# Low-rank attention followed by a maxout feed-forward on one Trainium2 core: the first batch's v in four loads, sums and copies in another order, the last product in narrower pieces

## The chip, the cores and the metric

The kernel runs on one core of one Trainium2 chip. A core has five engines with instruction queues of their own: TensorE (PE, with its weight loads shown apart as PEld), VectorE (DVE), ScalarE (ACT), GpSimd (POOL) and SyncE (SP). They meet through semaphores. DMA transfers are issued here by POOL (all loads of inputs) and by SP (E and F, the transposing transfers, and all stores). The metric is the device time of one execution in microseconds (us), given as the median of several runs.

## What is computed

For each of 8 batches and 8 heads, k and v (1024 rows of 64) are first projected to 64 rows with E and F; then comes ordinary softmax attention of q over those 64 rows. The result, as x with 8192 rows of 512, goes through a feed-forward layer with a two-way maximum:

```python
k_proj = np.einsum('ks,bhsd->bhkd', E, k)
v_proj = np.einsum('ks,bhsd->bhkd', F, v)
scores = scale * np.matmul(q, k_proj.transpose(0, 1, 3, 2))
attn = softmax(scores)
x = np.matmul(attn, v_proj)          # then heads side by side: 8192 x 512
g = np.maximum(x @ w1, x @ w2)       # 8192 x 1024
out = g @ w_out                      # 8192 x 512
```

## The kernel before

The maximum is taken as `max(x w1, x w2) = relu(x (w1 - w2)) + x w2`, so that `out = relu(x Wd) w_out + x (w2 w_out)`. `Wd = w1 - w2` (the tile `wd_sb`) and `M = w2 w_out` (the tile `m_sb`) are made once, while batch 0 is worked on; `M` is built by `m_steps`, seven products p1, p2, p6, p5, p7, p3, p4 with the additions of a Strassen-Winograd scheme. The same scheme with seven products is used for the two large products of every unit. A unit is half of a batch (512 rows), so there are 16 of them, numbered 0 to 15. `up_steps` makes `relu(x Wd)` of a unit in the tile `gt`; `down_steps` makes the unit's output. The scheme needs sums of blocks of its left operand: `sums_x` (of x) and `sums_g` (of gt), both at L590 and on DVE, and differences of blocks of its right operand (`T_sb`, L481, DVE, and `step_tw`).

Nothing is scheduled automatically. The order of the work on each engine is the order in which the program calls the steps: first the opening (batch 0's attention, written out line by line at the end), then a list `slots`, in which the up pieces of one unit alternate with the down pieces of the unit before. `at_slot(key, step, ...)` hangs further steps behind a slot. Slots (0, 10) to (0, 15) are the last up pieces of batch 0, slots (0, 16) to (0, 22) the seven steps of `m_steps`. Every engine works its own queue in order.

Loads of batch 0 are issued by POOL in this order: k, q, k, q of the first four heads and then of the last four, two heads at a time (L101); v, four heads at a time; then w2 and w1 in pieces (L124 and L133), `w_out` (L137), and batch 1's k, v, q and batch 2's k.

`step_kv` projects k or v with `eft`, the transposed E and F. For v of batch 0 it is called once for heads 0 to 3 and once for heads 4 to 7; each projection is written twice, to the lower and the upper 64 partitions of one PSUM bank. For batches 3 to 7 it is called for k and v of all heads together, and returns `finish_v`, which runs after the next slot: DVE copies v (L203), doubles the projected k (L205), SP then issues a transposing DMA that makes `kpt` (L230), and DVE copies v to the other half (L207). POOL waits on the doubled k (`step_gate`, L236) before it issues the loads of the next batch.

In the last unit (number 15) nothing runs beside the down products. There p4 is made in two halves of 128 output rows, each with an addition at L779 and a store of its own at L726.

Of the kernel before, what the change touches and what calls it, by code (L numbers as in the profile page):

```python
# [12 lines left out]
ALU = mybir.AluOpType  # L13
# [3 lines left out]
def kernel(  # L17
# [12 lines left out]
    nc = tc.nc  # L30

    B, H, S, D = q.shape
    KP = E.shape[0]
# [25 lines left out]
    def mm_bank(dtype=FP32, n=None):  # L59
        if n is None:  # L60
            n = turn.pop(0)
            turn.append(n)
        return ps.tile([128, 512 if dtype == FP32 else 1024], dtype, tag=f"mm{n}", name="mm_ps")
# [36 lines left out]
    def load(t, n, src, b, h0, h1):  # L100
        nc.gpsimd.dma_start(  # L101
            out=t[n][:, h0:h1],
            in_=src[b, h0:h1].rearrange("h (p c) d -> p h c d", c=NC),
        )
# [4 lines left out]
    for h0 in (0, H // 2):  # L109
# [3 lines left out]
        if h0 == 0:  # L113
            ident = const.tile([128, 128], FP32)
            make_identity(nc, ident)
    load(tiles[0], "v", v, 0, 0, H // 2)
    load(tiles[0], "v", v, 0, H // 2, H)

    w1_sb = big(1).rearrange("p (r f) -> p r f", r=NDC)
    w2_sb = big(2).rearrange("p (r f) -> p r f", r=NDC)  # L120
# [58 lines left out]
    def step_kv(t, h0=0, h1=H, which="kv", att=False, dma=False, copy=nc.vector.tensor_copy):  # L179
        kv_ps = att_banks()[:, 0, :] if att else mm_bank()  # L180
        n = (h1 - h0) * D
        both = which == "v"
        for c in range(NC):
            for w in which:
                i = "kv".index(w)
                for r in range(2) if both else (i,):
                    nc.tensor.matmul(  # L187
                        out=kv_ps[r * KP : (r + 1) * KP, 0:n],
                        lhsT=eft[:, i, c, :],
                        rhs=t[w][:, h0:h1, c, :],  # L190
                        start=(c == 0), stop=(c == NC - 1),
                    )
        fl = lambda ap: ap[:, h0:h1].rearrange("p h z d -> p (h z d)")
        zd = lambda ap: ap.rearrange("p (h d z) -> p h z d", d=D // 2, z=2)
        if "k" in which:
            eng = nc.vector.tensor_copy if which == "k" else nc.scalar.copy
            kp = t["kp"][:, h0:h1]
            eng(out=kp[:, :, 0, :], in_=kv_ps[0:KP, 0:n].rearrange("p (h d) -> p h d", d=D))
        if both:
            copy(out=t["vp"][:, h0:h1], in_=zd(kv_ps[:, 0:n]))  # L200
        elif "v" in which:
            def finish_v():
                nc.vector.tensor_copy(out=t["vp"][KP:128, h0:h1], in_=zd(kv_ps[KP:128, 0:n]))  # L203
                if dma:
                    nc.vector.tensor_copy(out=kp[:, :, 1, :], in_=kp[:, :, 0, :])  # L205
                    step_kpt_dma(t)
                nc.vector.tensor_copy(out=fl(t["vp"][0:KP]), in_=fl(t["vp"][KP:128]))  # L207

            if att:
                return finish_v  # L210
            finish_v()
# [17 lines left out]
    def step_kpt_dma(t):  # L229
        nc.sync.dma_start_transpose(  # L230
            out=t["kpt"], in_=t["kp"].rearrange("p h r d -> p (h r d)")
        )
# [226 lines left out]
    NX = NDC // 2  # L459
    CH = DM // 2  # L460
    units = [(b, o) for b in range(B) for o in range(2)]
    U = {(b, o): {"n": n, "b": b, "o": o, "t": tiles[b]} for n, (b, o) in enumerate(units)}

    T_sb = const.tile([128, 4, NG + NX, CH], FP16)
# [109 lines left out]
    def x_blk(u, j, h):  # L574
        return u["t"]["xt"][:, h * NX : (h + 1) * NX, j, u["o"] * W : (u["o"] + 1) * W]

    def g_blk(u, j, h):
        if u["b"] == 0:
            return u["t"]["gt", u["o"]][:, h * NG : (h + 1) * NG, j * W : (j + 1) * W]
        return u["gt"][:, h * NG : (h + 1) * NG, j * W : (j + 1) * W]  # L580
# [30 lines left out]
    def up_steps(u):  # L611
        for d in range(2):
            st = {}
            xbank, ybank = (2, 3) if d == 0 else (3, 2)

            def product(k, name, n, st=st, d=d):
                if n is not None:
                    st[name] = mm_bank(n=n)
                bank = st[name]
                X = lambda j, h: x_blk(u, j, h)  # L620
                Wb = lambda h, c: wd_sb[:, h * NX : (h + 1) * NX, c * HALF : (c + 1) * HALF]
                S = lambda i: s_x(i, u)
                a, w_ = {
                    1: lambda: (X(0, 0), Wb(0, 0)), 2: lambda: (X(0, 1), Wb(1, 0)),
                    3: lambda: (S(3), Wb(1, 1)), 4: lambda: (X(1, 1), t_w(3)),
                    5: lambda: (S(0), t_w(0)), 6: lambda: (S(1), t_w(1)), 7: lambda: (S(2), t_w(2)),
                }[k]()
                for m in range(2):
                    for n_ in range(NX):
                        nc.tensor.matmul(  # L630
                            out=bank[:, m * W : (m + 1) * W],
                            lhsT=w_[:, n_, (2 * d + m) * 128 : (2 * d + m + 1) * 128],
                            rhs=a[:, n_, :],
                            start=(n is not None and m == 0 and n_ == 0),
                            stop=(n_ == NX - 1), skip_group_check=True,
                        )
                return bank

            two = lambda ap: ap.rearrange("q (m n) -> q m n", m=2)

            def c_blk(j, c, d=d):
                return u["gt"][:, c * NG + 2 * d : c * NG + 2 * d + 2, j * W : (j + 1) * W]

            def add(j, c, x, y, c_blk=c_blk):
                nc.vector.tensor_tensor(out=c_blk(j, c), in0=two(x), in1=two(y), op=ALU.add)  # L645

            def relu(ap):
                nc.vector.tensor_scalar_max(ap, ap, 0.0)  # L648

            def p1(st=st, product=product, xbank=xbank, d=d):  # L650
                if d == 0:
                    new_gt(u)
                st["s1"] = keep("pu", product(1, "X", xbank))

            def p2(st=st, product=product, ybank=ybank, add=add, c_blk=c_blk):
                add(0, 0, product(2, "Y", ybank), st["s1"])
                relu(c_blk(0, 0))

            def p6(st=st, product=product):
                st["u1"] = keep("pu", product(6, "X", None))  # L660

            def p5(st=st, product=product, ybank=ybank):
                st["s5"] = keep("pu", product(5, "Z", ybank))

            def p7(st=st, product=product):
                st["u2"] = keep("pu", product(7, "X", None))

            def p3(st=st, product=product, add=add, d=d):
                add(0, 1, product(3, "Z", None), st["u1"])
                add(1, 1, st["u2"], st["s5"])  # L670
                relu(u["gt"][:, NG + 2 * d : NG + 2 * d + 2, :])

            def p4(product=product, c_blk=c_blk):
                bank = product(4, "X", None)
                UP_C21(out=c_blk(1, 0), in_=two(bank))

            yield from (p1, p2, p6, p5, p7, p3, p4)
# [6 lines left out]
    def down_steps(u, alone):  # L684
# [36 lines left out]
        def o_tile():  # L721
            return opool.tile([128, 2, CH], FP32, tag="o", name="o_sb")

        def store(j, c, o_sb, i0=0, i1=2):
            def issue():
                nc.sync.dma_start(  # L726
                    out=out.rearrange("(n p i o) m -> n o p i m", p=128, i=NI, o=2)[
                        b, j, :, 2 * o + i0 : 2 * o + i1, c * CH : (c + 1) * CH
                    ],
                    in_=o_sb[:, i0:i1],  # L730
                )

            if u["n"] < 2:
                held.append(issue)
            else:
                issue()
# [36 lines left out]
        def p4():  # L773
            o_sb = o_tile()
            if alone:
                for i in range(2):
                    bank = product(4, ("C", i), 2 + i, 6 * i, 6 * i + 6)
                    part = slice(i * CH, (i + 1) * CH)
                    nc.vector.tensor_tensor(  # L779
                        out=o_sb[:, i], in0=bank[:, part], in1=st["u2"][:, part], op=ALU.add,  # L780
                    )
                    store(1, 0, o_sb, i, i + 1)
                return
            nc.scalar.copy(out=o_sb, in_=two(whole(4, "X", None)))
            store(1, 0, o_sb)
# [87 lines left out]

    last = len(units) - 1
    for n, key in enumerate(units):
        downs = down_steps(U[key], n == last)
        if n in (0, last):
# [21 lines left out]

    for key, s_, *a in (
        *((10 + i // 2, sums_m, i) for i in range(4)), *((12 + i, step_t, 0, (i,)) for i in range(4)),
        (15, open_box, 0, 1, 2), (16, sums_x, U[0, 0], range(4)),
        (18, sums_g, U[0, 0], (0, 1)), (19, sums_g, U[0, 0], (2, 3)), (22, open_box, 3),
    ):
        at_slot((0, key), s_, *a)
# [123 lines left out]
```

## Time and profile before

| | |
|---|---|
| median of 5 runs | 324.71 us (324.42 to 326.69) |
| the profiled execution's own time | 324.86 us |
| its span, from the first to the last instruction | 323.1 us |
| TensorE clock granted | 1.0 throughout |
| PE busy | 314.8 us, 97% of the span |
| DVE busy | 236.7 us, 73% |
| ACT busy | 208.2 us, 64% |
| POOL busy | 42.1 us, 13% |

The span is 1.8 us shorter than the execution's own time; the rest lies around it. In a list of instructions in order of time, each line gives the start in us, the duration in us, the engine, the line of the kernel, the operation and its tiles; in brackets stands how long the engine was idle before and what ended the wait. The waits are given as the total in us, the number of times, and the longest. A busy share is an average: a share of 97% says nothing of where the rest was lost.

### The profile page before, as it was taken

What the parts mean: (1) busy time and instruction counts of PE and PEld (TensorE: products, weight loads), DVE (VectorE), ACT (ScalarE), POOL (GpSimd) and SP (SyncE); (2) the same over time, 40 slices, a digit from 0 to 9 for tenths busy, and PEclk for the clock granted to TensorE, in tenths of its full rate; (3) what the DMA queues carried; (4) which work ended last, traced back from release to release, by engine and by line L of the source; (5) the groups of instructions that cost most, each with busy time, mean ns of one, the idle gap of its engine ahead of it and who ended that gap; (6) DMA issues with size and microseconds to landing.
All of it is one profiled execution on the core that took longest, in us unless ns stands there. A gap on an engine that the chain in (4) does not pass through costs nothing.

```text
span 323.1 us, 9062 instructions
## 1 busy us (share of the span) xinstructions
PE 314.8 (97%) x3872; PEld 250.4 (77%) x3872; DVE 236.7 (73%) x419; ACT 208.2 (64%) x373; POOL 42.1 (13%) x65
## 2 busy tenths in 40 slices
PE   8979999999999999999999999999999999999995
PEld 3545587777887888878887888878887888888884
DVE  1356798886967796877967796977967796969572
ACT  1476842767776777667776777657776777765541
POOL 8649002003000400021000400030000000000000
PEclk9999999999999999999999999999999999999999
DMA  8999999998959999899989899889969131213033
GB/s 151 203 200 184 202 205 204 207 191 132 207 110 163 170 202 245 200 202 165 231 192 208 165 204 245 204 166 188 225 131 213 36 100 34 97 34 100 32 122 108
DMA packets 76280, 53.14 MB, mean 164 GB/s; under 512 B 29520, under 2 KB 76112, under 8 KB 76240
## 3 DMA queue, kind: packets, MB, share of 16 engines
q0 software_dynamic: 30976, 28.31, 55.9%
q1 hardware_dynamic: 45264, 24.25, 31.1%
q8 instruction: 30, 0.49, 0.6%
q14 instruction: 10, 0.08, 0.1%
HBM read 57.15 MB, written 16.78 MB: 229 GB/s over the span
## 4 chain that ended last, share of the span: by engine, by line
PE 84%; DMA 8%; POOL 4%; DVE 3%; issue 1%; ACT 0%; DVEq 0%; POOLq 0%
PE mm_ps L710 45%; PE mm_ps L630 26%; DMA v_sb<-in_v_dram 4%; PE att_ps L187 4%; DMA wo_sb<-in_moe_w_out_dram 3%; PE att_ps L285 3%; PE mm_ps L273 3%; POOL big L133 2%; PE mm_ps L518 1%; POOL q_sb L101 1%; POOL k_sb L101 1%; DVE T_sb L481 1%; DVE gt_sb L645 1%; PE mm_ps L244 1%; DVE big L590 1%
## 5 line engine op out<-in xcount | busy, mean ns | idle before, releaser
L604 ACT COPY p_sb<-mm_ps 128x512 f32<-128x512 f32 x180 | 102.0, 593 | 47.1 <-PE mm_ps L630 30.0
L710 PEld LDWEIGHTS <-big 128*128 128x128 f16 x768 | 73.4, 98 | 12.4 <-issue 3.9
L710 PE MATMUL mm_ps<-T_sb,big 128*128 128x256 f16 x576 | 78.0, 273 | 0.0
L645 DVE TENSOR_TENSOR gt_sb<-mm_ps,p_sb 128x512 f16<-128x512 f32 x56 | 38.5, 688 | 45.4 <-PE mm_ps L630 41.6
L630 PE MATMUL mm_ps<-big,big 128*128 128x256 f16 x336 | 50.4, 273 | 0.0
L630 PEld LDWEIGHTS <-big 128*128 128x128 f16 x448 | 43.8, 98 | 5.4 <-issue 0.2
L710 PEld LDWEIGHTS <-gt_sb 128*128 128x128 f16 x384 | 35.9, 98 | 9.4 <-issue 5.0
L710 PE MATMUL mm_ps<-wo_sb,gt_sb 128*128 128x256 f16 x256 | 43.0, 273 | 0.1
L630 PEld LDWEIGHTS <-wd_sb 128*128 128x128 f16 x336 | 32.9, 98 | 4.2 <-issue 0.4
L630 PE MATMUL mm_ps<-xt_sb,wd_sb 128*128 128x256 f16 x224 | 33.6, 273 | 0.2 <-ACT ex_sb L366 0.2
L366 ACT ACTIVATE ex_sb<-mm_ps 128x512 f16<-128x512 f32 x50 | 27.2, 596 | 9.7 <-PE att_ps L285 7.6
L392 DVE TENSOR_TENSOR xt_sb<-att_ps,ld_sb 128x1024 f16<-128x1024 f32 x26 | 31.7, 1218 | 0.1
L740 DVE TENSOR_TENSOR o_sb<-mm_ps,p_sb 128x512 f32<-128x512 f32 x32 | 21.9, 684 | 7.0 <-PE mm_ps L710 6.9
L236 POOL COPY junk<-qt_sb 1x1 f16<-1x1 f16 x6 | 1.5, 257 | 176.8 <-DMA qt_sb<-q_sb 176.8
L710 PE MATMUL mm_ps<-m_sb,xt_sb 128*128 128x256 f16 x128 | 24.4, 273 | 0.0
L680 ACT ACTIVATE gt_sb<-mm_ps 128x512 f16<-128x512 f32 x28 | 16.8, 600 | 9.5 <-PE mm_ps L630 9.5
L590 DVE TENSOR_TENSOR big<-gt_sb 128x1024 f16<-128x1024 f16 x32 | 21.9, 685 | 0.2
L648 DVE TENSOR_SCALAR gt_sb<-gt_sb 128x512 f16<-128x512 f16 (+1 forms) x56 | 20.5, 365 | 1.9
L710 PE MATMUL mm_ps<-T_sb,gt_sb 128*128 128x256 f16 x128 | 21.5, 273 | 0.0
L710 PE MATMUL mm_ps<-wo_sb,big 128*128 128x256 f16 x128 | 21.5, 273 | 0.0
L710 PEld LDWEIGHTS <-xt_sb 128*128 128x128 f16 x192 | 18.8, 98 | 2.2
L645 DVE TENSOR_TENSOR gt_sb<-p_sb 128x512 f16<-128x512 f32 x28 | 19.1, 681 | 0.0
(98 smaller groups left out, 430.2 us busy)
## 6 DMA issues: line engine op xcount, KB each, us to landing
out_dram<-o_sb SPq DMA_DIRECT2D x63, 256.0 KB, 2.8
k_sb<-in_k_dram POOLq DMA_DIRECT2D x7, 1024.0 KB, 9.7
v_sb<-in_v_dram POOLq DMA_DIRECT2D x7, 1024.0 KB, 15.9
q_sb<-in_q_dram POOLq DMA_DIRECT2D x5, 1024.0 KB, 22.8
q_sb<-in_q_dram POOLq DMA_DIRECT2D x4, 512.0 KB, 18.8
big<-in_moe_w_dram POOLq DMA_DIRECT2D x12, 128.0 KB, 8.4
k_sb<-in_k_dram POOLq DMA_DIRECT2D x4, 256.0 KB, 6.3
q_sb<-in_q_dram POOLq DMA_DIRECT2D x4, 256.0 KB, 7.4
```

The source lines that it names most:

```text
L187: nc.tensor.matmul(out=kv_ps[r * KP : (r + 1) * KP, 0:n], lhsT=eft[:, i, c, :], rhs=t[w][:, h0:h1, c, :], start=(c == 0), stop=(c == NC - 1),)
L273: nc.tensor.matmul(out=banks[e][pos : pos + Z, h * W : (h + 1) * W], lhsT=t["kpt"][o * D : (o + 1) * D, head, s * Z : (s + 1) * Z], rhs=t[ ...
L366: nc.scalar.activation(out=t["ex", g, j][:, e, :], in_=banks[e], func=ACTF.Exp, scale=scale)
L392: nc.vector.tensor_tensor(out=x_out(t, g, j).rearrange("q z o n -> q o z n"), in0=at_ps.rearrange("q o (z n) -> q o z n", z=2), in1=ld[:, ...
L590: nc.vector.tensor_tensor(out=S(i), in0=S(0) if x is None else x, in1=y(), op=op)
L604: copy(out=x, in_=bank)
L630: nc.tensor.matmul(out=bank[:, m * W : (m + 1) * W], lhsT=w_[:, n_, (2 * d + m) * 128 : (2 * d + m + 1) * 128], rhs=a[:, n_, :], start=(n ...
L645: nc.vector.tensor_tensor(out=c_blk(j, c), in0=two(x), in1=two(y), op=ALU.add)
L648: nc.vector.tensor_scalar_max(ap, ap, 0.0)
L680: nc.scalar.activation(out=out, in_=in_, func=ACTF.Relu)
L710: nc.tensor.matmul(out=bank[:, i * CH : (i + 1) * CH], lhsT=a(c)[:, i * 128 : (i + 1) * 128], rhs=w_(c), start=(n is not None and m == (lo ...
L740: nc.vector.tensor_tensor(out=o_sb, in0=two(x), in1=two(y), op=ALU.add)
```

## The change

Six edits. v of batch 0 is loaded two heads at a time, and `step_kv` projects v of batch 0 two heads at a time. In `finish_v` the doubling of k and the transposing DMA come ahead of the first copy of v. In the last unit the relu over the two lower blocks is made in two parts, one after each addition. The last unit's p4 makes its second half in two pieces of 128 columns, so that it has three additions and three stores. Two of the four sums of x of unit 0 are called at slot (0, 11), where they stood at slot (0, 16), and the other two at slot (0, 17).

```diff
-    load(tiles[0], "v", v, 0, 0, H // 2)
-    load(tiles[0], "v", v, 0, H // 2, H)
+    for h in range(0, H, 2):
+        load(tiles[0], "v", v, 0, h, h + 2)
...
-        for c in range(NC):
-            for w in which:
-                i = "kv".index(w)
-                for r in range(2) if both else (i,):
-                    nc.tensor.matmul(
-                        out=kv_ps[r * KP : (r + 1) * KP, 0:n],
-                        lhsT=eft[:, i, c, :],
-                        rhs=t[w][:, h0:h1, c, :],
-                        start=(c == 0), stop=(c == NC - 1),
-                    )
+        nh = 2 if both else h1 - h0
+        for h in range(0, h1 - h0, nh):
+            for c in range(NC):
+                for w in which:
+                    i = "kv".index(w)
+                    for r in range(2) if both else (i,):
+                        nc.tensor.matmul(
+                            out=kv_ps[r * KP : (r + 1) * KP, h * D : (h + nh) * D],
+                            lhsT=eft[:, i, c, :],
+                            rhs=t[w][:, h0 + h : h0 + h + nh, c, :],
+                            start=(c == 0), stop=(c == NC - 1),
+                        )
...
             def finish_v():
-                nc.vector.tensor_copy(out=t["vp"][KP:128, h0:h1], in_=zd(kv_ps[KP:128, 0:n]))
                 if dma:
                     nc.vector.tensor_copy(out=kp[:, :, 1, :], in_=kp[:, :, 0, :])
                     step_kpt_dma(t)
+                nc.vector.tensor_copy(out=t["vp"][KP:128, h0:h1], in_=zd(kv_ps[KP:128, 0:n]))
                 nc.vector.tensor_copy(out=fl(t["vp"][0:KP]), in_=fl(t["vp"][KP:128]))
...
                 add(0, 1, product(3, "Z", None), st["u1"])
+                if u["n"] == last:
+                    relu(c_blk(0, 1))
+                    add(1, 1, st["u2"], st["s5"])
+                    relu(c_blk(1, 1))
+                    return
                 add(1, 1, st["u2"], st["s5"])
                 relu(u["gt"][:, NG + 2 * d : NG + 2 * d + 2, :])
...
-                for i in range(2):
-                    bank = product(4, ("C", i), 2 + i, 6 * i, 6 * i + 6)
-                    part = slice(i * CH, (i + 1) * CH)
+                a = cat(g_blk(u, 1, 1), x_blk(u, 1, 1))
+                for i, m0, m1, n in (0, 0, CH, 2), (1, 0, CH // 2, 3), (1, CH // 2, CH, xbank):
+                    bank = mm_bank(n=n)
+                    for c in range(NG + NX):
+                        nc.tensor.matmul(
+                            out=bank[:, 0 : m1 - m0],
+                            lhsT=a(c)[:, i * 128 : (i + 1) * 128],
+                            rhs=T_sb[:, 3, c, m0:m1],
+                            start=(c == 0), stop=(c == NG + NX - 1),
+                        )
                     nc.vector.tensor_tensor(
-                        out=o_sb[:, i], in0=bank[:, part], in1=st["u2"][:, part], op=ALU.add,
+                        out=o_sb[:, i, m0:m1], in0=bank[:, 0 : m1 - m0],
+                        in1=st["u2"][:, i * CH + m0 : i * CH + m1], op=ALU.add,
                     )
-                    store(1, 0, o_sb, i, i + 1)
+                    store(1, 0, o_sb, i, i + 1, m0, m1)
...
-        (15, open_box, 0, 1, 2), (16, sums_x, U[0, 0], range(4)),
+        (11, open_box, 1), (11, sums_x, U[0, 0], (0, 1)),
+        (15, open_box, 0, 2), (17, sums_x, U[0, 0], (2, 3)),
```

`open_box(1)` takes over the memory of `w1` for the sums of x; `open_box(0, 2)` that of E and F and of `w2`.

More of the change, by code (lines that the diff above doesn't have):

```diff
@@ L461 @@
     units = [(b, o) for b in range(B) for o in range(2)]
+    last = len(units) - 1
     U = {(b, o): {"n": n, "b": b, "o": o, "t": tiles[b]} for n, (b, o) in enumerate(units)}
@@ L666, in p7, with p3 @@
                 st["u2"] = keep("pu", product(7, "X", None))
-            def p3(st=st, product=product, add=add, d=d):
+            def p3(st=st, product=product, add=add, c_blk=c_blk, d=d):
                 add(0, 1, product(3, "Z", None), st["u1"])
+                if u["n"] == last:
[3 more added lines that the diff above has]
+                    return
                 add(1, 1, st["u2"], st["s5"])
@@ L722, in o_tile, with store @@
             return opool.tile([128, 2, CH], FP32, tag="o", name="o_sb")
-        def store(j, c, o_sb, i0=0, i1=2):
+        def store(j, c, o_sb, i0=0, i1=2, m0=0, m1=CH):
             def issue():
@@ L727, in issue @@
                     out=out.rearrange("(n p i o) m -> n o p i m", p=128, i=NI, o=2)[
-                        b, j, :, 2 * o + i0 : 2 * o + i1, c * CH : (c + 1) * CH
+                        b, j, :, 2 * o + i0 : 2 * o + i1, c * CH + m0 : c * CH + m1
                     ],
-                    in_=o_sb[:, i0:i1],
+                    in_=o_sb[:, i0:i1, m0:m1],
                 )
@@ L872 @@
     slots = [((0, n), x) for n, x in slots]
-    last = len(units) - 1
     for n, key in enumerate(units):
```

## The prediction, made before the changed kernel was run

> **What bounds the kernel now.** I read the page's totals first, then busy time by stretches, then the waits, then the order of time where PE has gaps.
>
> ```profile
> PE 314.8 (97%) x3872; PEld 250.4 (77%) x3872; DVE 236.7 (73%) x419; ACT 208.2 (64%) x373; POOL 42.1 (13%) x65
> ```
>
> ```profile
> core 0: us, PE busy (x) PEld busy (x) DVE busy (x) ACT busy (x) POOL busy (x), PEclk, DMA share, GB/s
> ...
> 20.00:28.00 8.00, 6.93 (x123) 3.91 (x120) 6.66 (x12) 3.96 (x7) 6.14 (x10) 1.00 1.38 196
> 42.00:50.00 8.00, 7.41 (x69) 5.98 (x69) 7.49 (x14) 2.93 (x5) 0.00 (x0) 1.00 1.32 203
> 150.00:310.00 160.00, 159.90 (x1967) 134.22 (x1965) 124.15 (x221) 110.62 (x204) 6.85 (x12) 1.00 0.72 149
> ```
>
> PE is busy 159.90 us of the 160 us from 150 on: there nothing can be won without removing matmuls, and the change removes none. Only the opening, one hole at 42 us and the tail are left. The hole, as PE and DVE see it in order of time:
>
> ```profile
> 41.27 1.04 PE L518 MATMUL mm_ps<-T_sb,p_sb 128*128 128x256 f16 x8
> 42.90 1.91 PE L518 MATMUL mm_ps<-T_sb,p_sb 128*128 128x256 f16 x16 [0.59 <-DVE m_sb L531]
> ```
>
> ```profile
> 38.16 0.69 DVE L481 TENSOR_TENSOR T_sb<-wo_sb 128x1024 f16<-128x1024 f16 x1 [1.20 <-DMA wo_sb<-in_moe_w_out_dram]
> ...
> 40.09 0.68 DVE L481 TENSOR_TENSOR T_sb<-wo_sb,T_sb 128x1024 f16<-128x1024 f16 x1
> 40.70 0.42 DVE L590 TENSOR_TENSOR big<-xt_sb 128x512 f16<-128x512 f16 x1
> ...
> 41.83 0.42 DVE L590 TENSOR_TENSOR big<-xt_sb,big 128x512 f16<-128x512 f16 x1
> 42.16 0.69 DVE L531 TENSOR_TENSOR m_sb<-mm_ps,p_sb 128x512 f16<-128x512 f32 x1
> ```
>
> DVE idles 1.20 us for `w_out`, makes four differences, then four sums of x, and only then p2's addition, which frees the bank that p5 needs. PE waits for it. The opening, from POOL's list and the DMA issues:
>
> ```profile
> 19.39 0.72 POOL L133 DMA_DIRECT2D big<-in_moe_w_dram x1 [2.93 <-DMA v_sb<-in_v_dram]
> 21.92 2.15 POOL L133 DMA_DIRECT2D big<-in_moe_w_dram x3 [1.82 <-DMA v_sb<-in_v_dram]
> ```
>
> ```profile
> v_sb<-in_v_dram POOLq DMA_DIRECT2D x2, 512.0 KB, 12.4
> ```
>
> Each of POOL's loads, from the ninth on, waits for the landing of the load eight before it (the eleventh on q's first, the seventeenth on v's first). And the tail:
>
> ```profile
> 310.71 0.43 DVE L648 TENSOR_SCALAR gt_sb<-gt_sb 128x1024 f16<-128x1024 f16 x1
> 311.24 0.69 DVE L590 TENSOR_TENSOR big<-gt_sb 128x1024 f16<-128x1024 f16 x1
> ...
> 311.96 0.69 DVE L590 TENSOR_TENSOR big<-big,gt_sb 128x1024 f16<-128x1024 f16 x1
> ...
> 312.71 5.13 PEld L710 LDWEIGHTS <-big 128*128 128x128 f16 x48 [0.22 <-DVE big L590]
> ```
>
> In the last unit relu, sum and sum follow one another on DVE, and PE's p6 waits for the end of them.
>
> **The change part by part.**
>
> *Two sums of x sooner.* At slot 11 they fall into DVE's 1.20 us of idling before 38.16: two at 0.42 us, overlapping by 0.07, are 0.78 us. Cover: the wait for `w_out`; without it they would cost 0.78 us on DVE. The other two go behind p2's addition. DVE is then free at 40.77. The addition also needs ACT's copy of p1 (done 41.19) and p2, whose last matmul ends at 41.44 (40.40 plus eight at 0.109, plus 0.17 of pipeline). It starts at 41.47 and ends at 42.16; p5 starts at 42.20 in place of 42.90. **-0.70 us.** What is late next? DVE: sums_x 2 and 3 run to 42.95, the four sums of gt (0.61 apart) to 45.5, so p3's addition comes at 45.5 in place of 45.79 while PE gained 0.70. p2's addition of unit 0 (50.32) comes 0.2 sooner, and PE's p5 needs it only after p6 (50.95 plus 1.31, less 0.70): covered by 0.8. Then the landing of batch 1's v: issued 28.84, 19.4 us under way, it lands at 48.24; its projection starts at 49.10 and can come at most 0.84 sooner.
>
> *v in four loads, projected by twos.* POOL issues two more, at 0.72 us each, ahead of all weights: the first weight load goes from 9.34 to 11.89, the next three each take the place two later. Their landings (9.34 plus 12.9, 10.61 plus 12.3, 11.89 plus 11.7, 13.23 plus 11.1) stand 0.65 us apart where the issues stand 1.3 apart: the transfers queue, so the landing does not move with the issue. From the fourth L133 load on, which waits for the last piece of v at 21.63, POOL's times stay, and with them `w_out` at 26.96. Cover: that queue. Projection: the first pair of heads (landing about 1.3 us before the whole half) is done while the second is under way, so each projection ends half of its 0.87 us sooner, -0.43 us. DVE is busy without a gap from 21.28 to 26.82, but fourth in it stands wd's difference at 23.08, which needs w1's first load, landed 22.91. So the three products before it start 0.43 sooner, and the rest only 0.14: **-0.14 us** at 27.41, where PE's unbroken run begins.
>
> Here a rule speaks against the change. The nearest rows: 16 transposes of 128 columns (L244) take 1.06 us, about 56 ns each, and 16 of 64 columns into two column groups (L218) 0.44 us, 27 ns each. The Trainium skill (TensorE: Matmul & The Clock Gate, Back-to-back issue gap) gives about 81 ns per matmul of 128 columns in a real stream of weight loads and matmuls. By the rows the 32 matmuls of a half take 0.9 us, as 16 do now. By the page 2.6 us: from 18.87 they end at 21.5 in place of 20.2, and 1.2 us is lost in the opening, of which the hole at 42 gives back 0.76; the last product loses 12 x 25 = 0.3. The whole sum is -0.65 by the rows, +0.95 by the page. I take the rows.
>
> *k doubled ahead of v.* Per batch, five times: the doubling (0.29) and the transposing DMA start 0.69 sooner on DVE and SP, the copy of v 0.29 later; the sum is the same. PE waited for `kpt` once, and that cost 0.03 us (the run before it ends at 217.79, the scores start at 217.81). vp is read 3 us later, the bank is wanted at 109.66 and free at 106.7. On SP only stores stand behind it. POOL's gate opens up to 0.69 sooner, and the next loads with it, but the transposing DMA has moved by the same. 0, between -0.05 and +0.3 (a kpt late once per batch by the 0.7 us that its landing varies, less slack 0.4).
>
> *Relu in two.* Addition 309.38, relu of 512 (0.29) at 310.10, addition 310.32, relu 311.04, sum at 311.43 in place of 311.24: **+0.19 us** before p6, which has no slack. What it buys, gt's first block ready sooner for p2 at 311.19, was in time anyway. In the first half of that unit (302.85) DVE idles afterwards: 0.
>
> *Last product.* Twelve matmuls at 56 ns for six at 109: 0. The last addition shrinks from 0.42 to about 0.29 (the relu and copies of half size: 0.29), but DVE and SP (0.36 to 0.44 per issue, now five in a row) bring the last issue to 320.0, against 319.93. It decides nothing: the stores run at about 340 GB/s without a gap from 319.05 to 321.5, the last 768 KB queueing behind one another. No row has stores in pieces of 512 bytes; bounds are -0.13 (all of the shorter addition) and +0.39 (128 KB at half of that rate). Loads that write 512-byte pieces (L124, 0.65 us per 128 KB) keep the rate of 1-KB ones (1.28 per 256 KB): 0.
>
> Sum: -0.70 - 0.14 + 0.19 = **-0.65 us**, on the profiled execution's 324.86: 324.21. That execution lies 0.15 above the median of 324.71, so the median should become **324.1**.
>
> **The rivals.**
>
> *A, the gain is stopped.* If batch 1's v lands 0.8 us later than here, the projection at 49.10 stays where it is and only the relu's +0.19 is left: 324.9. For: one landing, at the end of a full queue, margin 0.02 us. Against: its place in the queue is untouched.
>
> *B, all transfers come sooner.* v's first half took 3.6 us after the last of q (15.5 to 19.1), the second 2.55; if weights shared the engines there, their later issue gives back up to 1.05 us to v, weights and batch 1 alike: -1.05 - 0.70 + 0.19, 323.1. Against: the rate was 200 GB/s throughout, so bytes would have to vanish.
>
> *C, slower: weights follow their issue.* If w1's first load lands 2.55 us later (25.5), DVE stands at wd's difference and everything behind it waits, PE's 27.41 too. The hole of 0.76 is absorbed: +2.45 - 0.76 + 0.19 = +1.9, 326.6. It decides once the queue runs dry, when a load lands less than about 5 us after its issue (the shortest here, 21.92 plus 5.1). Against: the shifted loads would still have 9 to 10 us.
>
> **How the numbers follow.** Within 0.5% is about what a measurement of this kernel can tell from no change: 323.09 to 326.33. The forecast (323.6 to 324.6) has 0.66, A 0.15, the page's matmul spacing (325.7) 0.03: same 0.84. B 0.09 is faster, C 0.07 slower. The range 323.2 to 325.3 holds the forecast and A, 0.81, and leaves out the rest.
>
> **What would show it.** Right: no wait of PE for L531 at 42 us, two L590 before 38.16, p2's addition near 41.3; v's pairs landing near 17.8, 19.1, 20.4 and 21.6; `w_out` still at 38.1; p6's wait in the last unit 0.2 longer; the last landing paced by the stores. Wrong: wd's first difference later than 23.1, the v matmuls at over 42 ns each (there the pairs lose what they gain), batch 1's projection waiting for v, or a wait for kpt in every batch.

## The result and the profile after

| | before | after |
|---|---|---|
| median, both kernels measured in turn on the same chips | 325.53 us (77 runs) | 324.31 us (42 runs, 323.42 to 327.12) |
| ratio to before | | 0.9972, 95% interval 0.9961 to 0.9983 |
| the profiled execution's own time | 324.86 us | 324.2 us |
| its span | 323.1 us | 322.4 us |

The changed kernel is a little faster: by 0.9 us by the ratio (0.6 to 1.3), by 0.7 us between the two profiled executions. Single executions scatter by more than that. After's lie in groups about 1 us apart (323.4 to 324.9, 325.2 to 325.5, 326.2 to 326.3, 327.1); what parts these groups no trace here shows. Some executions have a lone stretch of 3.4 us in which TensorE is granted half of its clock; where a trace shows one, this is said. The ratios leave out every run that took over 1.5% longer than the fastest of its kernel (8 of 22 for only_finish, 3 of 21 for best_old_v, one of before's), while the medians count all runs.

The totals of after, and its stretches:

```profile
PE 314.9 (98%) x3910; PEld 251.2 (78%) x3910; DVE 236.6 (73%) x422; ACT 208.2 (65%) x373; POOL 43.2 (13%) x67
```

```profile
core 0: us, PE busy (x) PEld busy (x) DVE busy (x) ACT busy (x) POOL busy (x), PEclk, DMA share, GB/s
...
20.00:28.00 8.00, 6.97 (x135) 3.88 (x128) 6.72 (x12) 4.00 (x8) 6.41 (x10) 1.00 1.38 197
...
42.00:50.00 8.00, 8.00 (x74) 6.50 (x73) 7.90 (x15) 2.93 (x5) 0.00 (x0) 1.00 1.32 204
...
150.00:310.00 160.00, 159.93 (x1970) 134.71 (x1968) 124.40 (x221) 111.11 (x205) 7.45 (x12) 1.00 0.74 150
```

PE now shows as busy through the whole of 42 to 50 us, where it lost 0.59 before. From 150 on it shows as busy as it was (159.93 of 160). Keep this row in mind: about half of what the change brought in the profiled execution lies in this stretch, and the busy share doesn't show it.

The place of the hole, on PE, among its weight loads and on DVE, in order of time:

```profile
41.42 2.92 PE L521 MATMUL mm_ps<-T_sb,p_sb 128*128 128x256 f16 x24
...
48.63 0.40 PE L189 MATMUL att_ps<-k_sb,eft 128*64 128x512 f16 x1
48.86 0.38 PE L189 MATMUL att_ps<-v_sb,eft 128*64 128x512 f16 x1
```

```profile
42.43 2.50 PEld L521 LDWEIGHTS <-p_sb 128*128 128x128 f16 x23 [0.15 <-issue]
```

```profile
23.10 0.43 DVE L435 TENSOR_TENSOR wd_sb<-big,big 128x512 f16<-128x512 f16 x1 [0.19 <-DMA big<-in_moe_w_dram]
...
37.02 0.42 DVE L593 TENSOR_TENSOR big<-xt_sb 128x512 f16<-128x512 f16 x1
37.47 0.43 DVE L593 TENSOR_TENSOR big<-big,xt_sb 128x512 f16<-128x512 f16 x1
38.66 0.69 DVE L484 TENSOR_TENSOR T_sb<-wo_sb 128x1024 f16<-128x1024 f16 x1 [0.76 <-DMA wo_sb<-in_moe_w_out_dram]
...
41.69 0.69 DVE L534 TENSOR_TENSOR m_sb<-mm_ps,p_sb 128x512 f16<-128x512 f32 x1 [0.41 <-PE mm_ps L521]
42.29 0.41 DVE L593 TENSOR_TENSOR big<-xt_sb 128x512 f16<-128x512 f16 x1
```

p6, p5 and p7 of `m_steps` are one row of 24 matmuls now. Two sums of x stand ahead of 38.66, and p2's addition waits for PE (0.41). PE in turn still waits for this addition, but only 0.15 us, inside the row, as its weight loads show. POOL's list in the opening:

```profile
12.10 0.72 POOL L124 DMA_DIRECT2D big<-in_moe_w_dram  x1 [0.56 <-DMA k_sb<-in_k_dram]
...
18.33 0.72 POOL L133 DMA_DIRECT2D big<-in_moe_w_dram  x1 [1.67 <-DMA v_sb<-in_v_dram]
19.36 0.72 POOL L133 DMA_DIRECT2D big<-in_moe_w_dram  x1 [0.31 <-DMA v_sb<-in_v_dram]
20.61 0.72 POOL L133 DMA_DIRECT2D big<-in_moe_w_dram  x1 [0.53 <-DMA v_sb<-in_v_dram]
21.89 2.15 POOL L133 DMA_DIRECT2D big<-in_moe_w_dram  x3 [0.56 <-DMA v_sb<-in_v_dram]
...
25.24 2.14 POOL L133 DMA_DIRECT2D big<-in_moe_w_dram  x3 [0.49 <-DMA big<-in_moe_w_dram]
```

Four waits for four pieces of v; at 21.89 (21.92 before) POOL is where it was. Then it waits 0.49 for the fourth weight load, which landed at 24.95 (24.33 before), and so it issues `w_out` at 27.38 (26.96 before) and batch 1's v at 29.13 (28.84 before). The tail:

```profile
309.22 0.29 DVE L651 TENSOR_SCALAR gt_sb<-gt_sb 128x512 f16<-128x512 f16 x1
309.43 0.68 DVE L648 TENSOR_TENSOR gt_sb<-p_sb 128x512 f16<-128x512 f32 x1
310.14 0.29 DVE L651 TENSOR_SCALAR gt_sb<-gt_sb 128x512 f16<-128x512 f16 x1
310.54 0.69 DVE L593 TENSOR_TENSOR big<-gt_sb 128x1024 f16<-128x1024 f16 x1
```

```profile
312.01 5.14 PEld L718 LDWEIGHTS <-big 128*128 128x128 f16 x48 [0.42 <-DVE big L593]
```

p6 of the last unit waits 0.42 where it waited 0.22.

To see where the 0.7 us came from, I laid the two traces over each other. ACT carries out the same instructions in the same order in both, so the start of one of them in after less its start in before is a curve of what has been won up to there:

| at (us of before) | 44 | 60 | 100 | 114 | 150 | 186 | 222 | 258 | 316 |
|---|---|---|---|---|---|---|---|---|---|
| after less before (us) | -0.47 | -0.28 | -0.27 | -0.39 | -0.51 | -0.64 | -0.76 | -0.89 | -0.70 |

PE's unbroken run begins 0.14 later (27.55 against 27.41), so the hole gave 0.61. Batch 1's v, for which PE waits between 48.63 and 48.86, takes 0.20 of it away between 44 and 100 us. Then, in five steps of 0.12 in the places of batches 3 to 7, another 0.62 is won, which the prediction had at nothing. The last unit costs 0.19. 0.14 - 0.61 + 0.20 - 0.62 + 0.19 = -0.70.

### The profile page after: what moved, and what is told of

It reads as the page before. It is cut to its first block, busy times and chain, and to the rows that moved or that the text cites. A ratio compares the mean times of both kernels' runs of the same rounds, so it can differ in the third digit from the quotient of the medians.

```text
span 322.4 us, 9145 instructions
## 1 busy us (share of the span) xinstructions
PE 314.9 (98%) x3910; PEld 251.2 (78%) x3910; DVE 236.6 (73%) x422; ACT 208.2 (65%) x373; POOL 43.2 (13%) x67
## 4 chain that ended last, share of the span: by engine, by line
PE 88%; DMA 5%; DVE 3%; POOL 1%; issue 1%; ACT 0%; DVEq 0%; POOLq 0%
PE mm_ps L718 44%; PE mm_ps L633 26%; PE mm_ps L419 4%; PE att_ps L189 4%; PE att_ps L287 3%; DMA big<-in_moe_w_dram 3%; PE mm_ps L275 3%; DMA k_sb<-in_k_dram 2%; PE mm_ps L521 2%; DVE gt_sb L648 1%; POOL k_sb L101 1%; DVE big L593 1%; PE mm_ps L246 1%; POOL q_sb L101 0%; PE mm_ps L788 0%
## 5 line engine op out<-in xcount | busy, mean ns | idle before, releaser
L718 PEld LDWEIGHTS <-gt_sb 128*128 128x128 f16 x376 | 35.1, 98 | 9.3 <-issue 5.0
L718 PE MATMUL mm_ps<-T_sb,gt_sb 128*128 128x256 f16 x120 | 20.3, 273 | 0.0
```

The source lines that it names most:

```text
L718: nc.tensor.matmul(out=bank[:, i * CH : (i + 1) * CH], lhsT=a(c)[:, i * 128 : (i + 1) * 128], rhs=w_(c), start=(n is not None and m == (lo ...
```

## The experiments

All but after were measured in five rounds, in four sessions. Before's own median differed between the sessions (324.89 to 325.53, after's included), so kernels of different sessions are compared by their ratios. The columns "at" give the curve above, taken from the one profiled execution of each kernel against before's: at 60 us it holds the opening, the landings and the hole, from 100 to 258 us the five batches, up to 316 us the last unit.

| kernel | median us | ratio to before, 95% | span | at 60 | at 258 | at 316 |
|---|---|---|---|---|---|---|
| after | 324.31 | 0.9972 (0.9961 to 0.9983) | 322.4 | -0.28 | -0.89 | -0.70 |
| only_sums | 324.09 | 0.9964 (0.9951 to 0.9976) | 322.3 | -0.82 | -0.82 | -0.82 |
| only_v | 325.64 | 1.0004 (0.9990 to 1.0018) | 322.6 | -0.56 | -0.54 | -0.53 |
| only_finish | 327.02 | 1.0030 (1.0011 to 1.0050) | 328.3 | +2.17 | +5.22 | +5.23 |
| only_tail | 325.68 | 1.0012 (0.9999 to 1.0025) | 324.3 | +0.89 | +0.92 | +1.12 |
| no_finish | 324.73 | 1.0000 (0.9983 to 1.0018) | 322.9 | -0.39 | -0.40 | -0.20 |
| twice_copy | 325.55 | 1.0012 (1.0002 to 1.0021) | 324.1 | -0.14 | +0.81 | +1.01 |
| late_copy | 323.61 | 0.9956 (0.9944 to 0.9969) | 322.1 | -0.13 | -1.23 | -1.02 |
| no_relu | 323.85 | 0.9966 (0.9949 to 0.9982) | 321.7 | -0.78 | -1.40 | -1.40 |
| best | 323.28 | 0.9948 (0.9920 to 0.9975) | 321.2 | -0.81 | -1.92 | -1.92 |
| best_old_v | 327.22 | 1.0052 (1.0035 to 1.0068) | 325.7 | -0.54 | +2.54 | +2.55 |
| best_old_product | 323.81 | 0.9942 (0.9922 to 0.9963) | 321.5 | -0.51 | -1.61 | -1.61 |
| old_v_gated | 324.12 | 0.9983 (0.9969 to 0.9997) | 321.5 | -0.80 | -1.67 | -1.66 |

The column "at 60" moves by half a microsecond between kernels whose openings are the same program (after, late_copy, no_relu and best: -0.28, -0.13, -0.78, -0.81): single landings differ that much from execution to execution. Only the changes along a row, from column to column, are read below.

**only_sums: the two sums of x sooner, alone, in the kernel before.**

```diff
-        (15, open_box, 0, 1, 2), (16, sums_x, U[0, 0], range(4)),
+        (11, open_box, 1), (11, sums_x, U[0, 0], (0, 1)),
+        (15, open_box, 0, 2), (17, sums_x, U[0, 0], (2, 3)),
```

> The kernel before with one edit: two sums of x of unit 0 at slot 11, the other two at slot 17. Prediction's theory: PE's wait for L531 at 42.9 us goes, 0.70 us there, and all of it is kept to the end: p6 of the last unit at about 312.0. Rival: the landing of batch 1's v (48.2 us in the profile before, 48.8 after) holds the projection, and only 0.2 to 0.5 us is left behind 51 us.

PE's run began at 27.20, 0.21 sooner than before, and PE's wait for p2's addition is down to the 0.15 us of after: -0.82 at 44 us, of which 0.61 is the hole. Batch 1's projection was not stopped here (k and v at 48.28), so all of it is kept to the end. By the ratio the edit wins 1.2 us (0.8 to 1.6); one pair of executions doesn't explain the rest.

**only_v: v of batch 0 in four loads, alone.** The edit is the first two hunks of the change.

> The kernel before with one edit: batch 0's v in four loads, and projected two heads at a time. Prediction's theory: DVE's products with 1/sum start 0.3 to 0.4 us sooner (21.28 before), PE's unbroken run 0.14 sooner (27.41 before), and w_out lands at 38.1 as before: 0 to -0.14 us. Rival: two more transfers in the queue make everything behind them later; w1's first piece lands 0.15 to 0.3 us later and w_out 0.3 to 0.5 later, measured from the landing of q's first load, so PE's run starts later than 27.41 and the hole at 42 grows: +0.2 to +0.6.

No gain that the comparison can tell, 1.0004. The profiled execution is 0.53 us ahead all the same, and this shows what the hole is. There `w_out` landed sooner (first `T_sb` at 37.60 in place of 38.16), PE's run began at 27.30, and with the old order of the sums the row of p6, p5 and p7 is nearly unbroken:

```profile
41.17 3.08 PE L520 MATMUL mm_ps<-T_sb,p_sb 128*128 128x256 f16 x24
```

It takes 3.08 us where after's takes 2.92, so 0.16 of the hole is left. The hole depends on the distance between one landing and PE's run. From the start of the run to the first `T_sb` it is 10.74 us in before and 10.29 here; in only_finish and only_tail, which have the old order too but began their run late, it is 9.46, the row takes 2.92 there, and nothing of the hole is left. With the sums sooner the row takes 2.92 even in after, where the distance is 11.10.

**only_tail: the relu in two and the last product in narrower pieces, alone.** The hunks of `p3`, `store` and `p4`.

> The kernel before with two edits: the last unit's relu in two parts, and its last product with three additions and three stores. Prediction's theory: relu +0.19 us before p6 of the last unit (DVE's wait of PE there 0.22 before, 0.42 now), last product 0, since the stores drain one behind another: +0.2 in all. Rival: the shorter last addition and smaller last store end the kernel sooner by 0.1 to 0.3, and the sum is 0 or a gain.

The curve goes from +0.92 to +1.12 in the last unit, as in after (-0.89 to -0.70). What stands at +0.89 from 44 us on comes from the opening of that execution: F landed 0.35 us later than in before, and a stretch at half clock followed, from 7.9 to 11.3 us.

**no_relu: after, with the last unit's relu in one again.**

```diff
-                if u["n"] == last:
-                    relu(c_blk(0, 1))
-                    add(1, 1, st["u2"], st["s5"])
-                    relu(c_blk(1, 1))
-                    return
```

> The changed kernel with the last unit's relu in one instruction again. Prediction's theory: PE's p6 in the last unit waits 0.22 in place of 0.42, the end comes 0.19 us sooner. Rival: the relu in two parts serves p2, which then waits, and the end is the same or later.

The step of the last unit is gone: -1.40 at 258 and -1.40 at 316. With only_tail, this pins the +0.19 on the relu (the medians alone could not: 0.9966 and after's 0.9972 overlap).

**no_finish: after, with the old order in `finish_v`.** The line of the first copy of v goes back ahead of `if dma:`.

> The changed kernel with the old order in finish_v. Bank theory: 0.6 us of what the change gained is lost again, in five steps of 0.12 at about 110, 146, 182, 218 and 254 us. Prediction's theory: nothing is lost.

All five steps are gone: -0.39 at 60 us, -0.40 at 258. So the new order wins the 0.6 us. By what, PE's weight loads show. First before, then after, in batch 3, in order of time:

```profile
109.89 0.10 PEld L273 LDWEIGHTS <-kpt_sb 64*32 64x32 f16 x3
110.22 0.13 PEld L273 LDWEIGHTS <-kpt_sb 64*32 64x32 f16 x13 [0.22 <-issue]
```

```profile
109.62 0.34 PEld L275 LDWEIGHTS <-kpt_sb 64*32 64x32 f16 x16
```

and the matmuls of the same scores, before, after and in no_finish:

```profile
110.00 0.62 PE L273 MATMUL mm_ps<-qt_sb,kpt_sb 64*32 64x256 f16 x16
```

```profile
109.73 0.50 PE L275 MATMUL mm_ps<-qt_sb,kpt_sb 64*32 64x256 f16 x16
```

```profile
109.61 0.62 PE L275 MATMUL mm_ps<-qt_sb,kpt_sb 64*32 64x256 f16 x16
```

Sixteen scores matmuls took 0.62, 0.50, 0.62 us. From the second to the third it is 0.21 from start to start in before and 0.09 in after, where the first two stand 0.004 apart. The third is the first that writes to a second bank of PSUM (the memory that takes the results of matmuls). DVE's addition that empties this bank, before and after:

```profile
109.48 0.68 DVE L645 TENSOR_TENSOR gt_sb<-mm_ps,p_sb 128x512 f16<-128x512 f32 x1
```

```profile
109.08 0.68 DVE L648 TENSOR_TENSOR gt_sb<-mm_ps,p_sb 128x512 f16<-128x512 f32 x1
```

It ends at 110.16 and 109.76; the third matmul starts at 110.21 and 109.82, some 0.05 us behind it. The profile calls the wait "issue"; it is a wait for DVE. And DVE's addition comes at the end of an unbroken stretch that begins with `finish_v`. Before and after:

```profile
104.96 0.69 DVE L740 TENSOR_TENSOR o_sb<-mm_ps,p_sb 128x512 f32<-128x512 f32 x1 [1.30 <-PE mm_ps L710]
105.69 0.69 DVE L203 CAST vp_sb<-att_ps 64x512 f16<-64x512 f32 x1
106.41 0.29 DVE L205 COPY kp_sb<-kp_sb 64x512 f16<-64x512 f16 x1
106.73 0.29 DVE L207 COPY vp_sb<-vp_sb 64x512 f16<-64x512 f16 x1
107.03 0.69 DVE L590 TENSOR_TENSOR big<-gt_sb 128x1024 f16<-128x1024 f16 x1
```

```profile
104.69 0.69 DVE L748 TENSOR_TENSOR o_sb<-mm_ps,p_sb 128x512 f32<-128x512 f32 x1 [1.30 <-PE mm_ps L718]
105.30 0.28 DVE L206 COPY kp_sb<-kp_sb 64x512 f16<-64x512 f16 x1
105.61 0.69 DVE L208 CAST vp_sb<-att_ps 64x512 f16<-64x512 f32 x1
106.34 0.29 DVE L209 COPY vp_sb<-vp_sb 64x512 f16<-64x512 f16 x1
106.64 0.69 DVE L593 TENSOR_TENSOR big<-gt_sb 128x1024 f16<-128x1024 f16 x1
```

The same instructions with the same durations take 2.07 us (104.96 to 107.03) before and 1.95 us after. The starts stand 0.73, 0.72, 0.32, 0.30 apart in the old order and 0.61, 0.31, 0.73, 0.30 in the new: after the addition of 0.69 us, the doubling of k may start at 0.61, before the addition has ended, where the copy of v had to wait until 0.73. The 0.12 us is the step. The Trainium skill (VectorE: DVE Perf Modes, Two Vector instructions with no wait between them) states a rule, which it calls a model, that gives just this: an instruction is held until all earlier ones have finished if it begins to read or to write at another group of 32 partitions than the last access to that memory did. The addition works from partition 0; the doubling of k reads and writes from partition 0 too, the copy of v from partition 64. By the rule all four are held in the old order, and all but the doubling in the new, as the starts show. No run here moved a copy to other partitions to test the rule by itself.

**twice_copy and late_copy: the same stretch made longer and shorter.** If DVE's stretch sets the scores, any copy put into it or taken out must show there. twice_copy makes DVE's lower copy of v twice; late_copy puts it off by eight slots, past the addition.

```diff
                 nc.vector.tensor_copy(out=fl(t["vp"][0:KP]), in_=fl(t["vp"][KP:128]))
+                if dma:
+                    nc.vector.tensor_copy(out=fl(t["vp"][0:KP]), in_=fl(t["vp"][KP:128]))
```

> The changed kernel with the last of finish_v's three copies on DVE done twice in batches 3 to 7 (0.29 us more on DVE each time, nothing else changed, the same values written again). Bank theory: DVE's stretch up to the addition that frees the bank sets PE, so each batch costs 0.2 to 0.3 us more, 1.0 to 1.5 in all, and PE's wait inside the scores grows from 0.09 to 0.3 to 0.4. Transposing-DMA theory: kpt lands as before, so nothing changes. Prediction's theory: DVE has 27% of idle time, nothing changes.

```diff
-                nc.vector.tensor_copy(out=fl(t["vp"][0:KP]), in_=fl(t["vp"][KP:128]))
+                def low():
+                    nc.vector.tensor_copy(out=fl(t["vp"][0:KP]), in_=fl(t["vp"][KP:128]))
+
+                def later(k):
+                    return low() if k == 0 else lambda: later(k - 1)
+
+                return later(8 if dma else 0)
```

> The changed kernel with the last of finish_v's three copies put off by eight slots in batches 3 to 7, behind the addition and the relu of that stretch. Bank theory: DVE reaches the addition 0.3 us sooner, PE's remaining wait of about 0.09 us per batch goes, 0.45 us in all; no more, since PE is then the bound. Transposing-DMA theory: 0.

Scores of batch 3 in twice_copy and in late_copy:

```profile
109.86 0.83 PE L277 MATMUL mm_ps<-qt_sb,kpt_sb 64*32 64x256 f16 x16
```

```profile
109.88 0.40 PE L281 MATMUL mm_ps<-qt_sb,kpt_sb 64*32 64x256 f16 x16
```

0.83 and 0.40 us; the third starts 0.42 and 0.003 behind the second. The addition ends at 110.23 in twice_copy, 0.05 ahead of the third matmul, and at 109.61 in late_copy, before the row begins:

```profile
109.55 0.68 DVE L650 TENSOR_TENSOR gt_sb<-mm_ps,p_sb 128x512 f16<-128x512 f32 x1
```

```profile
108.93 0.68 DVE L654 TENSOR_TENSOR gt_sb<-mm_ps,p_sb 128x512 f16<-128x512 f32 x1
```

twice_copy loses 0.95 us from 60 to 258, 0.19 a batch, which stands 0.31 per batch above after's -0.12: one copy of 0.29 us. late_copy wins 1.10, or 0.22 a batch: the whole gap, and no more, since PE has then nothing left to wait for. The series of gaps (0.42, 0.21, 0.09, none) with 0.83, 0.62, 0.50, 0.40 us for the scores follows DVE's stretch. A transposing DMA that landed sooner could not make it: twice_copy adds its copy behind that DMA's issue, and the gap stands before the third matmul and not before the first. The medians of one session go the same way: 323.61 for late_copy, 324.73 for no_finish, 325.55 for twice_copy.

**only_finish: the new order in `finish_v`, alone.** In the kernel before, the line of the first copy of v moves behind the `if dma:` block.

> The kernel before with one edit: in finish_v the doubling of k and its transposing DMA come ahead of the copy of v. The prediction's theory: the three DVE copies take the same time in either order and kpt was never late, so nothing changes (0, PE at p6 of the last unit still at about 312.7 us). Bank theory: in each of five batches the scores' second bank is freed by DVE's addition (L645), DVE's three copies take 2.07 us from the addition ahead of them to the sum behind them in the old order and 1.95 in the new, and PE's third score matmul waits for that: PE gains about 0.12 us per batch, 0.6 us in all, in five equal steps at about 110, 146, 182, 218 and 254 us. Transposing-DMA theory: the gain comes from kpt landing sooner; then the steps are there as well, but the wait behind them is the one for kpt.

The steps are there (+2.17, then +2.05, +1.91, +1.79 after batches 3, 4 and 5). The +2.17 comes from the opening: F landed 1.65 us later than in before, so that PE waited 1.41 for it, and a stretch at half clock followed, from 9.9 to 13.3 us. Then, in batch 6, it loses 3.6 us: the curve jumps to +5.35. PE waited 2.29 us for the transposing DMA of k there, and was then granted half clock for 3.4 us. The edit that wins 0.6 us in after makes the kernel before slower, 1.0030. Its times spread from 323.94 to 330.53, and the profiled one, 330.10, is the second longest: the curve shows what can happen here, not how often.

**best, best_old_v, old_v_gated: what saves the edit in after.** best is after with late_copy's edit and no_relu's, and so keeps all that was shown to win. best_old_v is best with v of batch 0 in two loads as before.

> The changed kernel with two edits: the last of finish_v's copies put off by eight slots in batches 3 to 7, and the last unit's relu in one instruction. If the two parts add up: 0.45 us by the copy and 0.19 by the relu, 0.6 under the changed kernel and about 1.4 under the kernel before. If PE is bound elsewhere once the bank comes free in time, only one of them shows.

> The same with batch 0's v in two loads and projected four heads at a time, as in the kernel before. Prediction's theory: 0.14 us slower than with v in four loads. Rival: v does not set PE's start at all, the landing of the weights does; then the two differ by no more than those landings differ between executions (up to 0.5 us either way), DVE's first product with 1/sum starts 0.3 later with two loads, and wd's first difference stays right behind the landing of w1's first piece in one and behind DVE's products in the other.

best wins 1.11 us from 60 to 258, loses nothing in the last unit, and is the fastest kernel here: 0.9948 of before. best_old_v goes with it up to 186 us (-0.54 to -1.20) and then loses 4 us in batch 6, as only_finish did; its fastest run took 325.30, best's 323.00. Weight loads of the scores, and stretches of that place, in best_old_v:

```profile
218.92 0.14 PEld L279 LDWEIGHTS <-kpt_sb 64*32 64x32 f16 x16 [2.61 <-DMA kpt_sb<-kp_sb]
```

```profile
217.00:219.40 2.40, 0.48 (x18) 0.27 (x19) 0.49 (x2) 0.00 (x0) 0.00 (x0) 1.00 1.16 184
219.40:222.80 3.40, 3.40 (x18) 2.42 (x17) 0.00 (x0) 2.18 (x5) 0.00 (x0) 0.50 1.23 202
```

and what SP and POOL issue there:

```profile
212.56 1.21 SPq L236 DMA_TRANSPOSE kpt_sb<-kp_sb  x1
```

```profile
212.90 0.88 POOL L101 DMA_DIRECT2D k_sb<-in_k_dram  x1 [0.34 <-PE mm_ps L637]
```

The transposing DMA lands 6.3 us after its issue, where in best the same one needs 2.7. POOL issued the next batch's k 0.34 us behind it. The prediction had said that POOL's gate moves by as much as the transposing DMA does; it didn't look at what else holds POOL. Beside the doubled k, POOL waits for an earlier transfer too (that of the q transposes), and this wait ended 3.1 to 3.5 us after the start of batch 6's projection in before, only_sums, only_finish, only_tail and best_old_v, which have v in two loads, and 4.0 to 4.3 us after it in every kernel with v in four. In before POOL stood at the gate of the doubled k, 4.36 us after the projection, so the load could not come sooner; the new order opens that gate at 3.5. Over all kernels and batches, a k load 0.34 us behind the transposing DMA goes with 6.0 and 6.3 us to land, 0.58 us behind with 2.7 to 3.4, 0.94 and more with 2.6 to 4.0.

To test this, old_v_gated lets POOL in best_old_v also wait for the upper copy of v, which DVE makes after the doubling:

```diff
+        at_slot(("U", n, 0, 6), lambda t=t: (nc.gpsimd.tensor_copy(
+            out=junk, in_=t["vp"][KP : KP + 1, H - 1, 1, 0:1]), None)[1])
```

> best_old_v with one copy more on POOL per batch (one element of the upper half of v), so that POOL issues the next batch's loads only after DVE's copy of v, about 1 us later. Collision theory: best_old_v is slow because in batch 6 the next k load is issued 0.34 us behind the transposing DMA of k, which then lands in 6.3 us in place of 2.7 and lets PE's scores wait 2.6 us; with the load at least 0.9 us behind it lands in under 3.5, the wait is gone, and the kernel is as fast as best within 0.3 us. Rival: the transposing DMA is late for another reason (stores or E's place in the queue), or v in two loads is slow in the opening; then the wait in batch 6 or the 2 to 4 us stay.

```profile
216.37 0.14 PEld L279 LDWEIGHTS <-kpt_sb 64*32 64x32 f16 x16 [0.29 <-DMA kpt_sb<-kp_sb]
```

The load follows 1.16 us behind, the transposing DMA lands in 4.0 us (I had expected under 3.5), PE waits 0.29 in place of 2.61, and two thirds of the loss are back: 0.9983 against 1.0052, 2.2 us. Against best's 0.9948 it is still 1.1 us slower, where I had allowed 0.3. Batch 6's step is 0.2 of that; where the rest lies is open (the lowest times, 323.11 and 323.00, are close).

**best_old_product: best with the last product as it was.** The hunk of `p4` is undone.

> The same with the last unit's last product as in the kernel before: two halves, two additions, two stores. Prediction's theory: nothing changes, since the last stores drain one behind another; from the start of p6 in the last unit to the end 10.4 us in both. Rival: the smaller last addition and store end the kernel sooner, then this one is 0.1 to 0.3 slower.

0.9942 (0.9922 to 0.9963) against 0.9948 (0.9920 to 0.9975): no worth of the narrower pieces shows. In best the last additions end at 317.86, in this one at 318.28; shifted by the curve's 0.31 that is 0.11 us sooner. The last store is not: it lands at 320.12 in best, and at 320.00 in this one with the same shift.

## Why the prediction was right, and where it was not

The forecast and its range held (324.1 forecast, 324.31 measured; -0.65 forecast, -0.7 found in the profiled executions), but in part by luck. Of the 0.84 that the opening and the hole were to give, 0.27 was there at 100 us; 0.62 came later, from the term that the prediction had put at nothing. The median agrees by some luck too: the forecast started from 324.71, and before's median in turn with after was 325.53. Two of its sums are slightly off, without changing the forecast: 18.87 plus 2.6 is 1.3 us behind 20.2, not 1.2, and from 48.24 to 49.10 batch 1's projection has 0.86 us of room, not 0.84.

**Two sums of x sooner** (-0.70): right in mechanism, in place and nearly in size, -0.61. p2's addition came at 41.69, where the step's 41.47 with PE's later start makes 41.61; both sums fell into the wait for `w_out`. The missing 0.09 is the 0.15 that PE still waits for this addition, where the step left 0.06. The prediction took the hole as a fixed 0.70; only_v, only_finish and only_tail showed that it depends on the distance between a landing and PE's run.

**v in four loads** (-0.14): not found. PE's run began 0.14 later in the profiled after. The step "the rest only 0.14" rested on w1's landing at 22.91. DVE's three products did start sooner (21.02 against 21.28), but `wd`'s difference stayed where it was, 23.10, now with a wait of 0.19 for the DMA. Everything before that difference is hidden by the transfer. In the twelve traces whose opening ran at full clock the run began between 27.20 and 27.89, with v in two loads or in four, so a gain of 0.14 could not have been told from a landing. POOL's times were as forecast up to 21.89; `w_out`, forecast to stay at 26.96, was issued at 27.38. Of the two prices for its matmuls, the row's 27 ns held and the page's 81 ns did not:

```profile
18.86 1.08 PE L189 MATMUL mm_ps<-v_sb,eft 128*64 128x128 f16 x32
```

32 matmuls in 1.08 us are 34 ns each, and 28 ns from start to start. The rule that spoke against the change didn't decide anything here.

**Rival A** (batch 1's v stops the gain) came in part. v landed at 48.82 and not at 48.24, and 0.20 of the 0.61 was stopped at 49 us. The prediction held that its place in the queue was untouched; POOL issued it 0.29 later, behind the wait for the fourth weight load, and it was under way 0.27 longer. In only_sums the projection ran at 48.28 and nothing was stopped.

**k doubled ahead of v** ("the sum is the same", 0, between -0.05 and +0.3): wrong. This is the step that failed. The sum of durations is the same; the sum of the distances between starts is 0.12 us smaller, five times over, and DVE's place behind it is on PE's path. The trace of before showed both. The two starts 0.73 apart beside others of the same kind 0.61 apart (the sums of gt, 0.61, are in the prediction's own text) hinted at the size, and the `[0.22 <-issue]` among the weight loads of the scores at the path. I read that gap as PE's own, because PE was 159.90 of 160 busy, and wrote that nothing could be won from 150 us on. A busy share counts a matmul row that stands waiting inside as busy. The other half of the step's argument, that POOL's gate moves with the transposing DMA, failed too, unseen in after: without the other edit it costs 3 to 4 us, over ten times the upper bound of +0.3 that I gave.

**Relu in two** (+0.19): right to 0.01, by its own steps, in after, only_tail and no_relu.

**Last product** (0): right. From p6's start to the end it took 10.38 us before and 10.43 after, inside the step's bounds; the twelve matmuls of 128 columns came at about 56 ns.

**Rivals B and C**: the rate stayed (197 GB/s in 20 to 28 us, 196 before), and `wd`'s difference stayed at 23.10. The first three weight loads did not follow their issue (they landed at 22.27, 23.01 and 23.64; 22.27, 22.94 and 23.63 before). The fourth did in part: it landed 0.62 later. Counted from the last landing of v, it came 2.7 us behind in all six traces with v in two loads, and over 3.1 us behind in four of the eight with v in four.

Open is why two more loads at the start should make the q transposes of batch 6 land some 0.8 us later, counted from that batch's projection, 200 us on. Thirteen of the fourteen traces sort by it (old_v_gated, with v in two loads, has 3.9 us), but no run took the cause apart.

## What to carry to other kernels

Add up the distances between starts, not the durations: an exchange of two instructions on one engine can change the sum, and it matters where another engine waits behind that stretch. A small "issue" gap inside a row of matmuls may be a wait for a PSUM bank; look for the instruction on another engine that ends just before it. And try each edit with the others taken out: here one that was worth nothing kept another from costing 3 us.

## What was not expected of the hardware

A transposing DMA that often lands in 2.7 us took 6.0 and 6.3 us in the two cases where a large load was issued 0.34 us behind it, and 4.0 us at most when the load came 0.58 us or more behind. In both cases PE waited 2.3 to 2.6 us and its granted clock was then 0.50 for one stretch of 3.4 us, with PE busy throughout it. That the wait brought on the lower clock is not shown, since no run parted the two; together, in best_old_v, they cost 4 us. Two copies on DVE, of 0.69 and 0.29 us, exchanged in order, moved the end of their stretch by 0.12 us, because one of them could start before the addition ahead of it had ended.
